# A transformer block with segmented attention: flips of the second layernorm by DMA for all of segment 0, a doubled tile written in one instruction, the gate inside the product, and a new timetable

## The chip, the cores and the metric

The kernel runs on one core of a Trainium2 chip. A core has TensorE (PE, matrix products into the eight PSUM banks), VectorE (DVE), ScalarE (ACT), GpSimd (POOL) and SyncE (SP, which issues DMAs), each with its own list of instructions that it works off in order; semaphores order them against each other. The metric is the time of one execution on the device in microseconds (us). The profile is one execution taken by the hardware profiler.

## The reference

One block on 2048 tokens of width 576, in bf16: attention, then an MLP of width 4608, both behind a layernorm and with a residual.

```python
q, k, v = x @ wq, x @ wk, x @ wv          # 32 heads of 18; 4 segments of 512 tokens
for s in range(4):                        # per segment, all heads
    p = softmax(qs @ ks.T * scale + causal_mask)
    a_dot = p @ vs
    a_mem = (phi(qs) @ M) / (phi(qs) @ z + 1e-6)
    o = g * a_mem + (1 - g) * a_dot       # g = sigmoid(beta), one number per head
    M, z = M + phi(ks).T @ vs, z + sum(phi(ks))
h  = x + concat(o) @ wo                   # x went through a layernorm before wq, wk, wv
h2 = h + gelu(layernorm(h) @ w1 + b1) @ w2 + b2
```

phi(t) is t + 1 for positive t and exp(t) otherwise. The memory M, z is empty in segment 0.

## The kernel before, in words

The 2048 tokens are four segments (s = 0 to 3) of four tiles of 128 tokens. The work of each segment goes through stages, and the letter and digits in front of a step's name give stage and segment (A1exp: an exp of stage A, segment 1). Where segment 0 is split, a third digit gives the tile (B01) or the pair of tiles (C00, C01).

- X (line 782): load of x, layernorm (line 733: stats, then rstd on GpSimd, then apply, which subtracts the mean and multiplies), and a transposed copy, by TensorE for the first pairs of tiles (line 771) and otherwise through DRAM and a transposing DMA ("flip", line 646).
- P (line 884): the products for q, k and v (line 865) and their eviction from PSUM (copy, line 652); for the memory phi(k) from ek (exp on ScalarE), rk (a clamp, line 932) and fk (line 934). q and k go to DRAM (qkst, line 918) and come back transposed (A1flip and so on). Within segment 0 the flips go from SBUF to SBUF.
- M (line 946): products and sums for the memory (macc, mblk).
- A (lines 1000 and 1130): scores (st, st0), exp on ScalarE, masks of the diagonal blocks (line 1196 on GpSimd, 1194 on VectorE; in segment 0 lines 1040 and 1037, with eight blocks in one instruction), the products with v (val), a transpose of the result on VectorE (valT), the reciprocal of the softmax sum and its multiplication by 1-g (rec2, lines 1218 to 1220), the product with the values (comb, line 1222) and the sum with the memory part (comb2). rg (line 1143) clamps q for phi(q); it stands on GpSimd.
- B (line 1244): the output projection (Po and Ro, line 826, in two halves that change banks between them, or "fused" into one where they follow each other), the residual (hadd), the second layernorm, and the transposed copy of its result. The tile xn2 has room for 2 x 576 columns: "tail" (line 1265) copies the 576 columns a second time behind the first, so that a flip gives nine blocks of 128 that hold each half of the rows twice. Tiles 2 and 3 of segment 0 and all tiles of segments 1 to 3 are flipped by DMA; tiles 0 and 1 of segment 0 are transposed on TensorE (line 777, steps B00T and B01T, 18 transposes in all, with four copies out of PSUM on VectorE), and there the tail copies 64 columns only.
- C (line 1286): the first MLP product (F1, lines 1312 and 1349; for segment 0 in two halves of 256 tokens, C00 and C01), eviction with the bias and gelu.
- D: the second MLP product (F2, line 1398), the residual with b2 (hc), the sum (oadd, line 1409) and the store.

The order is written out. TIMETABLE (line 22) gives each step, by name and number, its rank and its engine ("d 267": VectorE, rank 267; a row with one letter in front holds for all of its steps). The program builds all steps with their dependencies, sorts them by rank (schedule, line 402) and emits them in that order, so each engine's list is the ranks that carry its letter. The costs written beside each step (in us) and the tables OVER, PORT and SLIP only decide which buffer a step takes, by a model of the times. A DMA on SP waits in SP's list for what it reads, with all that stands behind it. The loads of x tiles 2 and 3 and of the q weights wait besides for a small copy, "gate" (line 724), that is made when the first half of x tile 0 has landed.

The functions that the change touches and those that call them:

## Time and profile before

| | |
|---|---|
| median of 3 runs | 449.36 us (448.22 to 450.42) |
| the profiled execution | 449.18 us, its span 447.5 us |
| HBM read and written | 37.36 MB and 10.29 MB |
| DMA issues of flips (transposing DMAs) | 54, all from SP |

In the rows of the profile a line begins with the line number of the kernel and the engine, then the operation, what it writes and what it reads ("bank<-xreg,w1g"), the shapes, and the count. Time behind a bar is busy time in all and the mean of one in ns; after a second bar stands how long the engine was idle just before and who ended that. PEld is the load of weights into TensorE, which overlaps the products.

### The profile page before, as it was taken

How to read it: one execution, taken by the hardware profiler on the slowest of the kernel's cores; microseconds unless marked ns; L12 is line 12 of the kernel's file. 1: busy time of each engine (PE TensorE's matmuls, PEld its weight loads, DVE VectorE, ACT ScalarE, POOL GpSimd, SP SyncE). 2: the span in 40 equal slices, each digit the busy share in tenths (PEclk: the TensorE clock that was granted, in tenths of full speed). 3: DMA queues.
4: the chain of work that ended last, by engine and by line, in shares of the span. 5: the costliest groups of instructions: out<-in, count | busy, mean ns of one | idle time of the engine just before them, and what ended most of it. 6: DMA issues, size and time to landing. Idle time of an engine off the chain costs nothing. (4 is left out here: it accounts for less than half of the span.)

```text
span 447.5 us, 12499 instructions
## 1 busy us (share of the span) xinstructions
PE 431.5 (96%) x5345; PEld 278.9 (62%) x5346; DVE 286.9 (64%) x623; ACT 301.2 (67%) x261; POOL 180.8 (40%) x319
## 2 busy tenths in 40 slices
PE   6987999899999999999999999999999999999997
PEld 4766677656776676664444766654447775445775
DVE  6899888999889877795678688773774322000012
ACT  6887999898978798775898977563787002566000
POOL 5683867668355833651235265520212111000001
PEclk9999999999999999999999999999999999999999
DMA  7669869999899944861657505404503281340001
GB/s 226 173 134 219 302 216 210 244 260 247 174 285 221 318 159 95 147 130 25 186 162 153 140 4 103 91 4 130 173 1 94 68 198 44 128 149 1 0 15 41
DMA packets 78344, 63.41 MB, mean 142 GB/s; under 512 B 62288, under 2 KB 70096, under 8 KB 78288
## 3 DMA queue, kind: packets, MB, share of 16 engines
q1 hardware_dynamic: 78144, 62.52, 54.9%
q8 instruction: 42, 0.69, 0.7%
q10 hardware_dynamic: 144, 0.09, 0.1%
q14 instruction: 14, 0.11, 0.1%
HBM read 37.36 MB, written 10.29 MB: 106 GB/s over the span
## 5 line engine op out<-in xcount | busy, mean ns | idle before, releaser
L1185 ACT ACTIVATE pt<-bank 128x2048 bf16<-128x2048 f32 x60 | 112.5, 1876 | 32.8 <-PE bank L1181 26.9
L1398 PEld LDWEIGHTS <-hT 128*128 128x128 bf16 x1152 | 110.5, 98 | 34.7 <-issue 6.6
L1312 PE MATMUL bank<-xreg,w1g 64*128 64x512 bf16 x972 | 107.2, 376 | 0.0
L1312 PEld LDWEIGHTS <-w1g 64*128 64x128 bf16 x972 | 46.3, 94 | 57.3 <-issue 2.8
L1398 PE MATMUL bank<-w_lo,hT 128*128 128x288 bf16 x576 | 77.8, 286 | 0.2 <-issue 0.2
L1398 PE MATMUL bank<-w,hT 128*128 128x288 bf16 x576 | 76.8, 286 | 0.6 <-DVE ot L1409 0.6
L1409 DVE TENSOR_TENSOR ot<-bank,hc 128x288 bf16<-128x288 f32 x32 | 14.3, 452 | 90.5 <-PE bank L1398 86.6
L873 PE MATMUL bank<-hT,xreg 64*128 64x288 bf16 x864 | 58.9, 283 | 4.8 <-DMA hT<-in_A_w_dram 2.1
L1196 POOL TENSOR_SCALAR_AFFINE_SELECT pt<-pt 128x512 bf16<-128x512 bf16 x67 | 45.1, 688 | 30.6 <-ACT pt L1185 30.3
L873 PEld LDWEIGHTS <-xreg 64*128 64x128 bf16 x864 | 42.8, 94 | 17.1 <-issue 8.5
L1317 ACT ACTIVATE hT<-bank,b_col 128x512 bf16<-128x512 f32 x36 | 22.6, 687 | 45.6 <-PE bank L1312 45.3
L1327 DVE TENSOR_SCALAR hT<-bank,b_col 128x512 bf16<-128x512 f32 x42 | 30.1, 742 | 21.4 <-PE bank L1312 20.2
L1384 POOL TENSOR_TENSOR hc<-h,b_bc 128x288 f32<-128x288 bf16 x16 | 12.4, 774 | 76.9 <-DVE ot L1409 76.9
L1027 ACT ACTIVATE pt<-bank 128x2048 bf16<-128x2048 f32 x20 | 37.5, 1877 | 6.2 <-PE bank L1024 5.5
L1349 PE MATMUL bank<-xreg,w1g 64*128 64x256 bf16 x648 | 38.6, 269 | 0.5 <-DVE qk_pad L662 0.3
L1349 PEld LDWEIGHTS <-w1g 64*128 64x128 bf16 x648 | 30.8, 94 | 7.0 <-issue 3.6
L1332 ACT ACTIVATE hT<-hT 128x8192 bf16<-128x8192 bf16 (+2 forms) x6 | 31.7, 5318 | 0.2 <-DVE hT L1327 0.2
L1325 ACT ACTIVATE hT<-bank,b_col 128x512 bf16<-128x512 f32 x30 | 19.5, 685 | 16.2 <-PE bank L1312 15.9
L1181 PE MATMUL bank<-qk 32*128 32x384 bf16 (+3 forms) x384 | 23.8, 300 | 1.6 <-DVE v_aug L662 0.9
L753 POOL TENSOR_SCALAR ln<-ln 128x1 f32<-128x1 f32 x32 | 8.8, 277 | 39.2 <-DVE ln L750 39.0
L1226 POOL TENSOR_TENSOR o_nat<-t,t 128x288 bf16<-128x288 f32 x13 | 10.6, 816 | 28.0 <-DVE t L1167 20.4
L1145 DVE SCALAR_TENSOR_TENSOR e<-e,r 128x512 bf16<-128x512 bf16 x24 | 18.9, 788 | 4.0 <-ACT e L1141 3.5
(119 smaller groups left out, 564.2 us busy)
## 6 DMA issues: line engine op xcount, KB each, us to landing
w1g<-in_B_w_dram SPq DMA_DIRECT2D x41, 576.0 KB, 4.4
qkd<-qk_pad SPq DMA_DIRECT2D x12, 512.0 KB, 4.8
w_lo<-in_B_w_dram SPq DMA_DIRECT2D x3, 864.0 KB, 6.6
w<-in_B_w_dram SPq DMA_DIRECT2D x3, 864.0 KB, 6.6
xb<-in_A_x_dram SPq DMA_DIRECT2D x16, 144.0 KB, 3.8
out_dram<-ot SPq DMA_DIRECT2D x15, 144.0 KB, 1.8
x<-in_A_x_dram SPq DMA_DIRECT2D x6, 320.0 KB, 4.5
xnd<-xn SPq DMA_DIRECT2D x10, 160.0 KB, 3.1
```

What stands on the lines that cost most here:

```text
L873: nc.tensor.matmul(out=c.t[:, w, 0:HALF], lhsT=xTb.t[r, k, ts], rhs=wt[r, k, :], start=(k == 0), stop=(k == ND - 1))
L1027: ex = add(ps, {"act": 1.88}, lambda e: nc.scalar.activation(out=pt.t[:], in_=st.t[:], func=ACT.Exp, scale=scale), [sc], pt, [st], table=" ...
L1181: nc.tensor.matmul(out=st.t[:, i, off:off + n_], lhsT=qk[rows, 1, kt * P:(kt + 1) * P], rhs=qk[rows, 0, kt * P:L], start=True, stop=True, ...
L1185: ex = add(ps, {"act": 1.88}, lambda e, st=st, pt=pt: nc.scalar.activation(out=pt.t[:], in_=st.t[:], func=ACT.Exp, scale=scale), [sc], pt, ...
L1196: nc.gpsimd.affine_select(out=blk, in_=blk, pattern=[[0, 4], [1, P]], compare_op=ALU.is_ge, fill=0.0, base=0, channel_multiplier=-1)
L1312: nc.tensor.matmul(out=cc[w].t[:], lhsT=w1.t[rows, k, q, :], rhs=x2T[s].t[rows, k, :], start=(k == 0), stop=(k == ND - 1))
L1317: ready_f[f + w] = [add(pf - 12, {"act": 0.68}, lambda e, f=f, w=w, cc=cc: nc.scalar.activation(out=hT[:, :, f + w, :], in_=cc[w].t[:].rea ...
L1325: nc.scalar.activation(out=dst, in_=src, func=ACT.Identity, bias=b)
L1327: nc.vector.tensor_scalar(out=dst, in0=src, scalar1=b, scalar2=None, op0=ALU.add)
L1332: ge = add(2.9, {"act": 0.42 * (f1 - f0) + 0.2}, lambda e, f0=f0, f1=f1: nc.scalar.activation(out=hT[:, :, f0:f1, :], in_=hT[:, :, f0:f1, ...
L1349: nc.tensor.matmul(out=cc[w].t[:, q * 2 * P:(q + 1) * 2 * P], lhsT=w1.t[rows, k, q, :], rhs=x2T[s].t[rows, k, ts], start=(k == 0), stop=(k ...
L1398: nc.tensor.matmul(out=c.t[:, 0:HALF], lhsT=hT[:, tl // 2, f, (tl % 2) * P:(tl % 2 + 1) * P], rhs=w2_c[ch][:, f - ch * WCH, hf * HALF:(hf ...
```

## The change

1. Tiles 0 and 1 of segment 0 are flipped by DMA as well: B00T, B01T and their copies go, B00flip and B01flip come.
2. The apply of the second layernorm writes both halves of the doubled tile in one instruction (twice=True: the input is read twice); all tail copies go. The apply may stand on GpSimd.
3. The multiplication by 1-g leaves rec2. On VectorE it is done within the product (scalar_tensor_tensor), on GpSimd it is an instruction of its own in front of the product.
4. rg and rk may stand on VectorE, the x applies on GpSimd; the masks of segment 0 are halved (four blocks in an instruction), and each half has its own engine.
5. A new timetable: nearly every rank is another, with new engines for small steps. The costs and the port model that choose the buffers are changed. By engine: 22 applies move to GpSimd (12 of x, 10 of h), 13 rg and 5 rk to VectorE, of the 32 half masks of segment 0 ten stand on VectorE.

The diff, cut to its core (of the timetable the rows that the text needs, of the numbers of the cost model nearly none):

```diff
-    "X00dma": "s 49 34 33",
-    "dma": "s 2 9 14 60 51 192 101 283",
-    "gate": "g 32",
-    "X1dma": "s 65 66 116 149",
+    "X00dma": "s 35 33 14",
+    "dma": "s 5 8 17 62 46 116 158 758",
+    "gate": "d 9",
+    "X1dma": "s 66 51 117 114",
...
-    "X01apply": "d 47 44",
-    "X1apply": "d 105 112 110 127",
+    "X01apply": "d52 g49",
+    "X1apply": "g 97 128 80 67",
...
-    "P1qkst": "s 263 209 313 314",
-    "A1flip": "s 341 426 349 410 501 502 529 632",
+    "P1qkst": "s 269 206 317 305",
+    "A1flip": "s 349 422 365 414 481 495 525 622",
...
-    "A00mask": "g 133 134 180 102",
-    "A02mask": "g 234 246 228 308",
+    "A00mask": "g113 d125 d111 g106 d120 d145 d156 g167",
+    "A02mask": "d252 g258 g259 g192 g225 d226 g298 d311",
...
-    "A1rg": "g 357 428 364 485 542 626 555 679",
+    "A1rg": "d375 g423 d366 g457 d592 g616 d623 d654",
...
-    "B00Po": "p 219",
-    "B00Ro": "p 223",
-    "B00T": "p 274 284",
-    "B00apply": "d 267",
-    "B00copy": "d 275 285",
-    "B00rstd": "g 266",
-    "B00tail": "g 273",
+    "B00Po": "p 222",
+    "B00Ro": "p 224",
+    "B00apply": "d 248",
+    "B00rstd": "g 238",
+    "B00flip": "s 249",
...
-    "B01Po": "p 225",
-    "B01Ro": "p 232",
-    "B01T": "p 276 286",
-    "B01apply": "d 256",
-    "B01copy": "d 277 287",
-    "B01rstd": "g 255",
-    "B01tail": "d 257",
+    "B01Po": "p 240",
+    "B01Ro": "p 245",
+    "B01apply": "g 273",
+    "B01rstd": "g 272",
+    "B01flip": "s 300",
...
-    "B1apply": "d 851 892 933 816",
-    "B2apply": "d 1213 1266 1292 1224",
+    "B1apply": "g 839 942 916 929",
+    "B2apply": "d1173 g1307 g1321 g1246",
...
-    "C00F1": "p 297 321 366 305 330 337 378 439 419",
-    "C00dma": "s 95 260 261 303 327 328 374 404 406",
+    "C00F1": "p 301 330 374 318 340 348 380 444 430",
+    "C00dma": "s 147 204 216 217 333 347 378 400 419",
...
-PARTS = dict(mask=1, apply=1, pq=1, fk=1, comb=1, comb2=1, memfin=1, hc=1, tail=1, swap=1)
-PORT = {"dve": PARTS, "pool": dict(PARTS, rg=1, rk=1, rstd=2, mblk=4, omg=4, gmz=1)}
+PORT = {"dve": dict(mask=(1, 0), pq=(1, 0), fk=(1, 0), comb=(1, 0), comb2=(1, 0), memfin=(1, 0), hc=(1, 0), rec0=(1, 0),
+                    apply=(1, 1), swap=(1, 1), rk=(1, 1), rg=(1, 1), mean=(1, 1), tail=(1, 1)),
+        "pool": dict(mask=(1, 0), pq=(1, 0), fk=(1, 0), apply=(1, 0), comb=(1, 0), comb2=(1, 0), memfin=(1, 0), hc=(1, 0), swap=(1, 0), rk=(1, 0), rg=(1, 0),
+                     rstd=(2, 0), mblk=(4, 0), omg=(4, 0), gmz=(1, 0), tail=(1, 0), memset=(1, 1), eps=(3, 1))}
...
-        def layernorm(prio, src, after, xsrc, dst_buf, dcost, extra=(), centred=None):
+        def layernorm(prio, src, after, xsrc, dst_buf, dcost, extra=(), centred=None, twice=False):
...
                 if centred is not None:
                     VEC[e].tensor_scalar(out=dst_buf.t[:, 0:w], in0=src(), scalar1=sm.t[:, mid:mid + 1], scalar2=None, op0=ALU.subtract)
                     return
-                VEC[e].tensor_scalar(out=dst_buf.t[:, 0:w], in0=src(), scalar1=sm.t[:, 12:13], scalar2=sm.t[:, 15:16], op0=ALU.subtract, op1=ALU.mult)
-            return add(prio, {"dve": dcost}, apply, (begun or [a, b]) + list(extra), dst_buf, [sm, xsrc], name="apply")
+                dst, frm = dst_buf.t[:, 0:w], src()
+                if twice:
+                    dst, frm = dst_buf.t[:].rearrange("p (n c) -> p n c", n=2), frm.unsqueeze(1).to_broadcast([P, 2, w])
+                VEC[e].tensor_scalar(out=dst, in0=frm, scalar1=sm.t[:, 12:13], scalar2=sm.t[:, 15:16], op0=ALU.subtract, op1=ALU.mult)
+            cost = {"dve": dcost} if centred is not None else {"dve": dcost, "pool": 1.28 if twice else 0.75}
+            return add(prio, cost, apply, (begun or [a, b]) + list(extra), dst_buf, [sm, xsrc], name="apply")
 
 
         xnT, xn_ok, applied = {}, {}, []
...
-                    b = add(p0 - 0.2, {"pool": 0.67}, lambda e, rk=rk, pad=pad: nc.gpsimd.tensor_scalar(
+                    b = add(p0 - 0.2, {"pool": 0.67, "dve": 0.36}, lambda e, rk=rk, pad=pad: VEC[e].tensor_scalar(
                         out=rk.t[:], in0=pad.t[:, :, 1, :, 0:Dh], scalar1=BIG, scalar2=0.0, op0=ALU.min, op1=ALU.max), ks, rk, [pad], name="rk")
-                    f = add(p0 - 0.2, {"dve": 0.78}, lambda e, ek=ek, rk=rk, fk=fk: nc.vector.scalar_tensor_tensor(
+                    f = add(p0 - 0.2, {"dve": 0.76}, lambda e, ek=ek, rk=rk, fk=fk: nc.vector.scalar_tensor_tensor(
...
                 for u in range(0, len(diag), 2):
-                    o0, w = diag[u][4], diag[u][3]
-
-                    def mask(e, o0=o0, w=w):
-                        blk = pt.t[:, :, o0:o0 + 2 * w].rearrange("p i (b q) -> p i b q", q=w)[:, :, :, 0:P]
-                        if e == "dve":
-                            nc.vector.tensor_tensor(out=blk, in0=blk, in1=tri[:].unsqueeze(1).unsqueeze(1).to_broadcast([P, 4, 2, P]),
-                                                    op=ALU.mult)
-                        else:
-                            nc.gpsimd.affine_select(out=blk, in_=blk, pattern=[[0, 4], [0, 2], [1, P]], compare_op=ALU.is_ge, fill=0.0,
-                                                    base=0, channel_multiplier=-1)
-                    masks[u] = add(ps, {"dve": 0.87, "pool": 1.17}, mask, [ex, tri_ok], None, [pt], name="mask")
-                    masks[u].bias = {"dve": MASK_BIAS}
+                    for i0 in (0, 2):
+                        o0, w = diag[u][4], diag[u][3]
+
+                        def mask(e, o0=o0, w=w, i0=i0):
+                            blk = pt.t[:, i0:i0 + 2, o0:o0 + 2 * w].rearrange("p i (b q) -> p i b q", q=w)[:, :, :, 0:P]
+                            if e == "dve":
+                                nc.vector.tensor_tensor(out=blk, in0=blk, in1=tri[:].unsqueeze(1).unsqueeze(1).to_broadcast([P, 2, 2, P]),
+                                                        op=ALU.mult)
+                            else:
+                                nc.gpsimd.affine_select(out=blk, in_=blk, pattern=[[0, 2], [0, 2], [1, P]], compare_op=ALU.is_ge, fill=0.0,
+                                                        base=0, channel_multiplier=-1)
+                        masks[u, i0] = add(ps, {"dve": 0.43, "pool": 0.64}, mask, [ex, tri_ok], None, [pt], name="mask")
+                        masks[u, i0].bias = {"dve": MASK_BIAS}
                 return [(4 * Q + b, kt, q0, n_, off, pt) for (b, kt, q0, n_, off) in units], [ex] + list(masks.values())
 
             def values(tag, t0, parts, banks, acq, cost):
...
-                a = add(prio - 0.2, {"dve": 0.48}, c0, [a] + later, r1, [t1], name="rec")
...
-                b = add(pg, {"pool": 0.64}, lambda e, g=g, rb=rb: nc.gpsimd.tensor_scalar(
+                b = add(pg, {"pool": 0.62, "dve": 0.30}, lambda e, g=g, rb=rb: VEC[e].tensor_scalar(
...
 
                 def c0(e, g=g, r1=r1, t1=t1):
                     nc.vector.reciprocal(out=r1.t[:], in_=t1.t[:, :, Dh])
-                    nc.vector.tensor_scalar(out=r1.t[:], in0=r1.t[:], scalar1=omg_q[:, g:g + 1], scalar2=None, op0=ALU.mult)
-
-                def c1(e, r1=r1, t1=t1):
-                    VEC[e].tensor_tensor(out=t1.t[:, :, 0:Dh], in0=t1.t[:, :, 0:Dh], in1=r1.t[:].unsqueeze(2).to_broadcast([P, 16, Dh]), op=ALU.mult)
-                a = add(pc, {"dve": 0.53}, c0, [a] + later, r1, [t1], name="rec2")
-                a = add(pc, {"dve": 0.48, "pool": 0.70}, c1, [a], None, [r1, t1], name="comb")
-                a = add(pc, {"dve": 0.52, "pool": 0.87}, lambda e, g=g, t1=t1: VEC[e].tensor_tensor(
+
+                def c1(e, g=g, r1=r1, t1=t1):
+                    rb = r1.t[:].unsqueeze(2).to_broadcast([P, 16, Dh])
+                    if e == "dve":
+                        nc.vector.scalar_tensor_tensor(out=t1.t[:, :, 0:Dh], in0=t1.t[:, :, 0:Dh], scalar=omg_q[:, g:g + 1], in1=rb, op0=ALU.mult, op1=ALU.mult)
+                        return
+                    nc.gpsimd.tensor_scalar(out=r1.t[:], in0=r1.t[:], scalar1=omg_q[:, g:g + 1], scalar2=None, op0=ALU.mult)
+                    nc.gpsimd.tensor_tensor(out=t1.t[:, :, 0:Dh], in0=t1.t[:, :, 0:Dh], in1=rb, op=ALU.mult)
+                a = add(pc, {"dve": 0.26}, c0, [a], r1, [t1], name="rec2")
+                a = add(pc, {"dve": 0.46, "pool": 0.90}, c1, [a] + later, None, [r1, t1], name="comb")
+                a = add(pc, {"dve": 0.46, "pool": 0.82}, lambda e, g=g, t1=t1: VEC[e].tensor_tensor(
                     out=o_q(on)[:, :, Dh * g:Dh * g + Dh], in0=t1.t[:, :, 0:Dh], in1=t2s[g].t[:, :, 0:Dh], op=ALU.add),
                     [a, t2_ok[g]] + done[:1], on if g == 0 else None, [t1, t2s[g]] + ([on] if g else []), name="comb2")
                 done.append(a)
...
                         out=h.t[:, cs], in0=c.t[:, 0:HALF], in1=xb.t[:, cs], op=ALU.add), [a, ld, prev], h if hf == 0 else None,
                         [c, xb] + ([] if hf == 0 else [h]), name="hadd")
                 xn2 = Buf(xn2_s)
-                ap = layernorm(p0, lambda h=h: h.t[:], [prev], h, xn2, 0.48, later)
-                by_dma = s > 0 or tl in DMA_FLIP_0
-                w = D if by_dma else 64
-                ap = add(p0, {"pool": 0.72, "dve": 0.38} if by_dma else {"pool": 0.29, "dve": 0.22},
-                         lambda e, xn2=xn2, w=w: VEC[e].tensor_copy(out=xn2.t[:, D:D + w], in_=xn2.t[:, 0:w]), [ap], None, [xn2], name="tail")
+                ap = layernorm(p0, lambda h=h: h.t[:], [prev], h, xn2, 0.60, later, twice=True)
                 h_ok[t] = h, prev
-                if by_dma:
-                    x2_ok[s].append(flip(p0, lambda tl=tl: x2T[s].t[:, :, tl * P:(tl + 1) * P], lambda xn2=xn2: xn2.t[:], ND,
-                                         [ap] + (x2_ok[s][:1] if tl else p3_done), None if tl else x2T[s], [xn2] + ([x2T[s]] if tl else [])))
-                else:
-                    even = transposes(p0, xn2, [ap], lambda tl=tl: x2T[s].t[:, 0:KT, tl * P:(tl + 1) * P],
-                                      x2T[s] if tl == 0 else None, [] if tl == 0 else [x2T[s]])
-                    if tl:
-                        even.after.append(x2_ok[s][0][0])
-                    odd = transposes(p0, xn2, [ap], lambda tl=tl: x2T[s].t[:, KT:ND, tl * P:(tl + 1) * P], None, [x2T[s]], ND - KT, c0=64)
-                    odd.after.append(even)
-                    x2_ok[s].append([even, odd])
+                x2_ok[s].append(flip(p0, lambda tl=tl: x2T[s].t[:, :, tl * P:(tl + 1) * P], lambda xn2=xn2: xn2.t[:], ND,
+                                     [ap] + (x2_ok[s][:1] if tl else p3_done if s else []), None if tl else x2T[s], [xn2] + ([x2T[s]] if tl else [])))
 
         f2_chunks = {}
         last_w1 = [None]
...
-        DMA_FLIP_0 = (2, 3)
...
```

More of the change, by code (lines that the diff above doesn't have):

```diff
@@ L477, in schedule, with meet @@
         return order
+    @staticmethod
+    def meet(e, kind, other):
+        dve, pool = (kind, other) if e == "dve" else (other, kind)
+        return bool(dve) or not pool
     @staticmethod
```

43 lines of the change are left out of this document (22 added, 21 removed), and 527 rows, old and new, of the table TIMETABLE.

## The prediction

> **What bounds the kernel now.** I read the page's head and then the table of busy time by stretches (columns: stretch, its length, then busy us and instructions of PE, PEld, DVE, ACT and POOL, the granted clock, the DMA share and GB/s).
>
> ```profile
> span 447.5 us, 12499 instructions
> PE 431.5 (96%) x5345; PEld 278.9 (62%) x5346; DVE 286.9 (64%) x623; ACT 301.2 (67%) x261; POOL 180.8 (40%) x319
> ...
> 0.00:120.00 120.00, 108.14 (x1913) 77.47 (x1913) 106.61 (x235) 103.84 (x97) 79.97 (x157) 1.00 0.88 221
> 120.00:440.00 320.00, 318.99 (x3402) 198.16 (x3400) 178.99 (x385) 197.34 (x165) 100.06 (x161) 1.00 0.45 115
> 440.00:447.50 7.50, 4.38 (x36) 3.26 (x34) 1.28 (x3) 0.00 (x0) 0.73 (x1) 1.00 0.10 32
> ```
>
> TensorE is the bound: of 16.0 us in which it has nothing, 11.9 lie in the first 120 us (120.00 - 108.14), 1.0 in the next 320 and 3.1 at the end (the last addition and the store). The clock is 1.00 throughout. VectorE and ScalarE are nearly full in that first stretch (106.6 and 103.8 of 120) and have room later. The chain of waits, in order of time, says the same of the last part:
>
> ```profile
> 373.92 35.07 PE bank L1312 x324
> 408.99 35.40 PE bank L1398 x288
> ```
>
> Product follows product with nothing between. So an edit late in the kernel gains only where it takes instructions off TensorE, and an edit early gains what it takes out of the waits before 120 us. Those are in the waits of TensorE (total, times, longest):
>
> ```profile
> PE bank L873 <- DMA hT<-in_A_w_dram: 2.1, 1, 2.1
> PE bank L873 <- DVE qk_pad L662: 1.8, 3, 1.0
> PE bank L1024 <- DVE MZacc L968: 1.7, 1, 1.7
> ...
> PE bank L1024 <- ACT pt L1027: 1.3, 4, 0.4
> PE bank L1181 <- DVE v_aug L662: 0.9, 1, 0.9
> ...
> PE bank L873 <- DVE v_aug L662: 0.5, 1, 0.5
> ...
> PE bank L1349 <- DVE qk_pad L662: 0.3, 1, 0.3
> ```
>
> One wait is for weights at the start. Five rows are waits for VectorE to empty a bank: 1.8 + 1.7 + 0.9 + 0.5 + 0.3 = 5.2 us.
>
> **The transposes of tiles 0 and 1.** They go from TensorE to DMA flips.
>
> ```profile
> 55.56 1.27 PE L777 MATMUL bank<-ident,xn 128*128 128x128 bf16 x18
> 56.76 0.61 PE L1056 MATMUL bank<-pt,v_aug 128*19 128x256 bf16 x16
> 57.67 0.40 PE L1024 MATMUL bank<-w_lo 32*128 32x256 bf16 x8 [0.30 <-ACT pt L1027]
> ```
>
> The 18 transposes hold the engine from 55.56 to 56.76: 1.20 us, and the value step after them does not depend on them. Lower bound 0.9: the step at 57.67 already waits 0.30 for an exp, and would meet it earlier. Since TensorE is full afterwards, the gain is kept. I take **-1.2**. Changes between the ways of cutting the array (64 rows, 32 rows, 32 columns, whole) cost TensorE nothing net: counting them in both lists gives 215 before and 215 after, with four fused output projections in both.
>
> **VectorE before 120 us.** The rows are groups by form (busy us, mean ns) and, for the x apply, minimum, median and maximum of one:
>
> ```profile
> L765 DVE TENSOR_SCALAR xn<-x,ln 128x640 bf16<-128x640 bf16 x14 | 9.3, 670 | 0.6 <-POOL ln L754 0.5
> L765 DVE TENSOR_SCALAR xn<-h,ln x16: 348/428/837, 52.6 to 365.4; 128x576 bf16<-128x576 bf16 x16
> L765 DVE TENSOR_SCALAR xn<-x,ln x14: 392/442/1231, 9.4 to 99.6; 128x640 bf16<-128x640 bf16 x14
> L1220 DVE TENSOR_SCALAR r<-r,omg_q 128x16 f32<-128x16 f32 x24 | 7.0, 290 | 0.9
> L662 DVE COPY xreg<-bank 128x640 bf16<-128x640 bf16 x5 | 2.3, 483 | 0.8 <-PE bank L777 0.8
> L1194 DVE TENSOR_TENSOR pt<-pt,tri 128x512 bf16<-128x512 bf16 x29 | 14.9, 527 | 1.1 <-ACT pt L1185 1.1
> L1037 DVE TENSOR_TENSOR pt<-pt,tri 128x1024 bf16<-128x1024 bf16 x2 | 1.4, 678 | 0.0
> L1266 POOL COPY xn<-xn 128x576 bf16<-128x576 bf16 x7 | 4.8, 689 | 5.4 <-DVE xn L765 5.4
> ```
>
> I counted both lists up to the first product of C01. Off VectorE: 12 of the 14 x applies (12 x 0.67 = 8.0), two h applies (2 x 0.43 = 0.9), four copies after the transposes (4 x 0.45 = 1.8), three masks of A1 (3 x 0.53 = 1.6), four multiplications by 1-g (4 x 0.29 = 1.2): 13.5. Onto it: ten half masks of segment 0, priced as the A1 mask, which is as large, for two whole ones (10 x 0.53 - 2 x 0.68 = 3.9), and seven of the small clamps rg and rk, priced as the nearest row, the h apply (7 x 0.43 = 3.0): 6.9. Net about -6.6 of 106.6, so its idle time in the stretch grows from 13.4 to about 20 us. The gate multiplied within the product costs VectorE at least nothing more (the same 128 x 288 elements) and at most the 0.29 that it saves; from GpSimd's side it is one more 128 x 16 instruction where the product stands there.
>
> GpSimd takes the 12 x applies at about 0.77 each (the 0.689 of its 576-wide copy, times 640/576): an estimate. It is busy for 80 of the 120 us, so it has the room. A doubled apply lies between one and two of the plain ones: 0.43 to 0.86 on VectorE, 0.7 to 1.4 on GpSimd, where it replaces apply and tail together; I take 0.6 and 1.3. Late, in segments 1 to 3, both engines have idle time and TensorE does not wait for them, so I put all that at nothing; its cover is the 320 us stretch with 1.0 us of TensorE idle, and without that cover each doubled apply on GpSimd would cost its flip 0.9.
>
> What this buys is read at two waits, in the order of time of VectorE and of TensorE:
>
> ```profile
> 22.72 2.28 DVE L765 TENSOR_SCALAR xn<-x,ln 128x640 bf16<-128x640 bf16 x2
> 24.92 0.74 DVE L662 CAST qk_pad<-bank 128x576 bf16<-128x576 f32 x1
> ...
> 25.72 2.38 PE L873 MATMUL bank<-hT,xreg 64*128 64x288 bf16 x36 [1.00 <-DVE qk_pad L662]
> ...
> 28.92 1.28 PE L873 MATMUL bank<-hT,xreg 64*128 64x288 bf16 x18 [0.48 <-DVE v_aug L662]
> ```
>
> Two x applies, stretched to 1.14 us each, stand in front of the eviction that TensorE waits for. They leave the engine, so I count these waits as gone: 1.48. Of the other 3.7 I take a quarter, 0.9, between nothing and the half by which the idle time grows. Sum **-2.4**, bounds 0 and -5.2. What is late next is ScalarE: it keeps its work (and gets two swaps more) and its 1.3 us row of waits stays.
>
> The clamp A1rg on VectorE waits for the flips of A1; behind it in VectorE's list stand the eviction P1copy.8, a reciprocal and the evictions of C00, for whose banks TensorE waits. The flips are issued well ahead, so I put this at nothing; its bound is in the range.
>
> **The order of the first loads.** The second part of the k weights (the third load of the list "dma") is put behind the x tile 3, and that one waits for the gate.
>
> ```profile
> 1.73 0.90 SPq L640 DMA_DIRECT2D hT<-in_A_w_dram  x2
> 3.62 0.80 SPq L640 DMA_DIRECT2D x<-in_A_x_dram  x2
> 4.46 0.43 SPq L640 DMA_DIRECT2D hT<-in_A_w_dram  x1
> ...
> hT<-in_A_w_dram SPq DMA_DIRECT2D x1, 288.0 KB, 4.4
> ...
> 11.01 2.38 PE L873 MATMUL bank<-hT,xreg 64*128 64x288 bf16 x36 [2.06 <-DMA hT<-in_A_w_dram]
> ```
>
> Today it leaves at about 2.2. Behind the gate it leaves at about 4.0 and lands at 8.4, so the second half of the first k projection waits for some 1.2 us. That fits into the 2.06 us wait for the q weights. But these leave one issue (0.43) later. I take **+0.3**, bounds 0 and +0.9: the v weights are behind an x load of segment 1 too.
>
> **The flips of tiles 0 and 1 on the path to the first product of C00.**
>
> ```profile
> 47.91 0.66 PE L832 MATMUL bank<-wt_o,oT 64*128 64x288 bf16 x8
> 52.62 0.38 DVE L765 TENSOR_SCALAR xn<-h,ln 128x576 bf16<-128x576 bf16 x1
> 54.34 0.43 DVE L765 TENSOR_SCALAR xn<-h,ln 128x576 bf16<-128x576 bf16 x1 [0.37 <-POOL ln L754]
> 58.00 2.14 PE L1349 MATMUL bank<-xreg,w1g 64*128 64x256 bf16 x36
> ...
> xreg<-xn SPq DMA_TRANSPOSE x14, 3.6
> ```
>
> From the start of the last output projection of tile 1 to the first product of C00 pass 10.1 us today. The new list has a projection more in between and no transposes, about the same. The new chain is 5.1 us to the end of the earlier apply, or 6.9 to the end of the later one, then 3.6 for the flip, and up to 0.9 for the longer apply on GpSimd: 8.7 to 11.4. So the product waits between nothing and 1.3 us: I take **+0.3**.
>
> **Sum.** 449.18 us is the profiled execution's own time (span 447.5): 449.18 - 1.2 - 2.4 + 0.3 + 0.3 = 446.2. The median of the three runs, 449.36, is 0.18 above the profiled one, so the forecast is **446.4 us**.
>
> **Rivals.** *The larger gain*: all of the 5.2 us goes and neither new wait shows: 449.36 - 1.2 - 5.2 = 443.0. For it: four of the five rows are single waits, which a new order can remove whole. Against: ScalarE, at 103.8 of 120, keeps its pace.
>
> *The relief is eaten*: the x apply has a median of 442 ns and a maximum of 1231, and the two at 22.72 ran beside GpSimd. If the applies on GpSimd hold VectorE up in their turn, each meeting costs 1.23 - 0.44 = 0.79; from eight meetings on, among the 14 applies that go there early, the 6.6 us are used up. Then 449.36 - 1.2 + 0.6 = 448.8. The Trainium skill (SBUF — State Buffer, section SBUF: two separate sides) says that VectorE in its two-port forms and GpSimd take a shared port pair as an exclusive lock for a whole instruction; by that rule this rival would hold, and the 1231 ns agree with it. Against the rival: the applies that ran into this on VectorE are the ones that leave it.
>
> *Slower*: the flip of tile 1 becomes the wait. Its apply stands on GpSimd behind two masks of A02, and an rstd and an apply of X2, then its own rstd. A GpSimd instruction beside VectorE is stretched too:
>
> ```profile
> L1040 POOL TENSOR_SCALAR_AFFINE_SELECT pt<-pt x14: 1101/1112/1617, 18.7 to 75.6; 128x1024 bf16<-128x1024 bf16 x14
> ```
>
> With 0.5 us more (1.617 - 1.112) for each of six instructions, the wait in front of C00's first product becomes 1.3 + 3.0 = 4.3. On SP the two stores of P1, a load of X3, two of w1 and the first flip of A1 stand behind that flip, so the scores of segment 1 are late as well and the relief is not collected: 449.36 - 1.2 + 0.3 + 4.3 = 452.8. It decides from a wait of 3.1 us on.
>
> **How the numbers follow.** About 0.5% (2.25 us) is what a measurement of this kernel can tell from no change: below 447.1 is faster, above 451.6 slower. Forecast 0.52, larger gain 0.10, relief eaten 0.25, slower 0.13. Of the forecast's 0.52 I put 0.42 below 447.1 and 0.10 above. Faster 0.42 + 0.10 = 0.52; same 0.10 + 0.25 = 0.35; slower 0.13. The range leaves out the slower rival and half of the larger gain: 443.0 to 450.2.
>
> **What would show it.** In the changed profile: no transposes between the scores of A02 and the first product of C00; PE busy about 430.3; VectorE in the first 120 us near 100; the rows L662 of TensorE's waits at about half; the x applies on GpSimd at 0.75 to 0.8, or at 1.2 and more if the relief is eaten; the first product of C00 preceded by a wait below 1.3 for a DMA into xreg. I am wrong if TensorE's idle time before 120 us is still 11 us or more, or if new waits appear after 120 us.

## The result and the profile after

The changed kernel takes 479.44 us (median of 4 runs, 477.80 to 482.65) against 449.75 for the kernel before on the same chips: a ratio of 1.067, with an interval from 1.061 to 1.074. The forecast was 446.4 with a range up to 450.2, so it missed by 33 us and in sign. The profiled execution took 477.8 us, its span 476.1.

The head of the page:

```profile
span 476.1 us, 12461 instructions
PE 439.2 (92%) x5328; PEld 283.2 (59%) x5328; DVE 295.2 (62%) x583; ACT 303.2 (64%) x267; POOL 245.5 (52%) x338
```

The table of busy time by stretches (its columns as in the prediction):

```profile
0.00:120.00 120.00, 99.47 (x1681) 69.90 (x1682) 91.06 (x204) 92.40 (x92) 96.44 (x155) 0.94 0.80 198
120.00:440.00 320.00, 306.75 (x3384) 187.14 (x3383) 198.44 (x366) 209.54 (x174) 147.62 (x182) 0.99 0.44 124
```

GpSimd went from 180.8 to 245.5 us. VectorE's busy time rises too, from 286.9 to 295.2, though it has 40 instructions fewer; a row below shows why. TensorE idles for 20.5 us of the first 120 (11.9 before) and for 13.3 of the next 320 (1.0 before). VectorE and ScalarE do less before 120 us, not more (91.1 and 92.4, from 106.6 and 103.8): they wait, like TensorE. The granted clock is below 1 in both stretches. GpSimd's own groups by form say where its 65 us come from:

```profile
L766 POOL TENSOR_SCALAR xn<-h,ln 128x1152 bf16<-128x1152 bf16 x10 | 43.4, 4336 | 0.7
L766 POOL TENSOR_SCALAR xn<-x,ln 128x640 bf16<-128x640 bf16 x12 | 30.3, 2525 | 1.1
```

An x apply takes 2.53 us there and a doubled one 4.34. The prediction had 0.77 and 1.3. The 22 applies sum to 73.7 us instead of 22. In the waits of TensorE (total, times, longest) two kinds are new, waits for GpSimd and waits for a VectorE that is itself late because of GpSimd:

```profile
PE bank L1210 <- POOL pt L1199: 4.6, 5, 1.3
PE bank L1059 <- DVE qk_pad L660: 4.4, 1, 4.4
PE bank L779 <- POOL xn L766: 3.6, 1, 3.6
...
PE bank L1306 <- DMA xreg<-xn: 0.9, 1, 0.9
```

The last row is a flip of a later segment, at 324 us. The first product of C00 (L1343, at 65.87) did not wait for its flips here: it comes right behind the gap of 4.4 us, so this trace does not test the 0 to 1.3 of the prediction. The order of time shows both new kinds:

```profile
30.25 2.52 POOL L766 TENSOR_SCALAR xn<-x,ln 128x640 bf16<-128x640 bf16 x1
...
32.83 0.37 PE L779 MATMUL bank<-ident,xn 128*128 128x128 bf16 x3 [3.60 <-POOL xn L766]
...
57.43 4.29 POOL L766 TENSOR_SCALAR xn<-h,ln 128x1152 bf16<-128x1152 bf16 x1
58.05 4.73 DVE L935 TENSOR_SCALAR rk<-qk_pad 128x576 bf16<-128x576 bf16 x1
...
61.66 0.95 POOL L634 MEMSET MZ_blk<- 128x1024 bf16 x1
...
64.36 1.03 PE L1059 MATMUL bank<-pt,v_aug 128*19 128x256 bf16 x16 [4.39 <-DVE qk_pad L660]
```

At 30.25 TensorE's transposes wait directly for an x apply. At 57.43 a doubled apply starts; a clamp that VectorE otherwise does in some 0.3 us starts 0.6 later and ends at 62.78, when the apply (to 61.72) and the memset behind it (to 62.61) are over. I call this a hold. The eviction behind the clamp is late, and TensorE with it. After both gaps the granted clock falls. In short stretches (the clock is the third number from the end) it is 1.00 while TensorE has little or nothing to do, and 0.50 as soon as it works again:

```profile
28.00:32.00 4.00, 1.11 (x27) 0.82 (x25) 1.86 (x4) 3.78 (x4) 3.81 (x5) 1.00 1.27 138
34.00:36.00 2.00, 2.00 (x18) 1.03 (x14) 1.78 (x5) 0.00 (x0) 2.00 (x4) 0.50 1.22 268
60.00:62.00 2.00, 0.00 (x0) 0.00 (x0) 2.00 (x1) 0.75 (x1) 2.00 (x2) 1.00 0.00 0
66.00:68.00 2.00, 2.00 (x22) 1.36 (x20) 1.22 (x6) 2.00 (x2) 2.00 (x3) 0.50 0.59 229
```

My first theory after this was: the applies on GpSimd are too dear, and they cost time by holding VectorE up. The rival: they cost time because GpSimd itself gets late with all that stands behind them. A second rival: not the applies, but the new order.

### The profile page after: what moved, and what is told of

It reads as the page before. It is cut to its first block, busy times and chain, and to the rows that moved or that the text cites. A ratio compares the mean times of both kernels' runs of the same rounds, so it can differ in the third digit from the quotient of the medians.

```text
span 476.1 us, 12461 instructions
## 1 busy us (share of the span) xinstructions
PE 439.2 (92%) x5328; PEld 283.2 (59%) x5328; DVE 295.2 (62%) x583; ACT 303.2 (64%) x267; POOL 245.5 (52%) x338
## 5 line engine op out<-in xcount | busy, mean ns | idle before, releaser
L1306 PEld LDWEIGHTS <-w1g 64*128 64x128 bf16 x972 | 47.6, 94 | 58.8 <-issue 5.1
L1392 PE MATMUL bank<-w,hT 128*128 128x288 bf16 x576 | 78.3, 288 | 1.1 <-DVE t L1164 0.8
L1199 POOL TENSOR_SCALAR_AFFINE_SELECT pt<-pt 128x512 bf16<-128x512 bf16 x74 | 51.8, 714 | 41.6 <-ACT pt L1188 41.4
L1311 ACT ACTIVATE hT<-bank,b_col 128x512 bf16<-128x512 f32 x36 | 22.4, 688 | 47.9 <-PE bank L1306 47.8
L1378 POOL TENSOR_TENSOR hc<-h,b_bc 128x288 f32<-128x288 bf16 x11 | 8.3, 756 | 82.0 <-DVE ot L1403 82.0
L766 POOL TENSOR_SCALAR xn<-h,ln 128x1152 bf16<-128x1152 bf16 x10 | 43.4, 4336 | 0.7
L1321 DVE TENSOR_SCALAR hT<-bank,b_col 128x512 bf16<-128x512 f32 x39 | 27.6, 739 | 23.5 <-PE bank L1306 18.6
L1343 PE MATMUL bank<-xreg,w1g 64*128 64x256 bf16 x648 | 40.4, 278 | 0.1
L1343 PEld LDWEIGHTS <-w1g 64*128 64x128 bf16 x648 | 31.6, 97 | 7.6 <-issue 3.0
L1319 ACT ACTIVATE hT<-bank,b_col 128x512 bf16<-128x512 f32 x33 | 20.8, 685 | 19.7 <-PE bank L1306 19.6
L766 POOL TENSOR_SCALAR xn<-x,ln 128x640 bf16<-128x640 bf16 x12 | 30.3, 2525 | 1.1
```

The source lines that it names most:

```text
L766: VEC[e].tensor_scalar(out=dst, in0=frm, scalar1=sm.t[:, 12:13], scalar2=sm.t[:, 15:16], op0=ALU.subtract, op1=ALU.mult)
L1199: nc.gpsimd.affine_select(out=blk, in_=blk, pattern=[[0, 4], [1, P]], compare_op=ALU.is_ge, fill=0.0, base=0, channel_multiplier=-1)
L1306: nc.tensor.matmul(out=cc[w].t[:], lhsT=w1.t[rows, k, q, :], rhs=x2T[s].t[rows, k, :], start=(k == 0), stop=(k == ND - 1))
L1311: ready_f[f + w] = [add(pf - 12, {"act": 0.68}, lambda e, f=f, w=w, cc=cc: nc.scalar.activation(out=hT[:, :, f + w, :], in_=cc[w].t[:].rea ...
L1321: nc.vector.tensor_scalar(out=dst, in0=src, scalar1=b, scalar2=None, op0=ALU.add)
L1343: nc.tensor.matmul(out=cc[w].t[:, q * 2 * P:(q + 1) * 2 * P], lhsT=w1.t[rows, k, q, :], rhs=x2T[s].t[rows, k, ts], start=(k == 0), stop=(k ...
```

## The experiments

**All applies back on VectorE**, and then only the x or only the h applies, at the same ranks (the program picks the buffers anew from its cost model, so a few of these may differ as well):

```
-    "X1apply": "g 97 128 80 67",
+    "X1apply": "d 97 128 80 67",
...
-    "B1apply": "g 839 942 916 929",
+    "B1apply": "d 839 942 916 929",
```

> All 22 applies that the change put on GpSimd stand on VectorE again, at the same ranks; everything else is the changed kernel. Theory (price of the apply): on GpSimd it takes 2.52 us (x) and 4.34 us (doubled h) instead of my 0.77 and 1.3, and holds VectorE meanwhile; without that the time falls from 479 to 446-450, and TensorE's idle time to about 16 us. Rival (order): the new order itself is worse and the long applies only show up in it; then 465 or more.

Measured 449.14 us, 1.0007 times the kernel before (0.9987 to 1.0028): the loss is gone, and so the order by itself is not the cause. TensorE idles for 15.4 us (447.0 - 431.6), as expected. But nothing is left of the gain either.

> Only the 12 x applies go back to VectorE; the 10 doubled h applies stay on GpSimd. TensorE's time beyond its products and changes of mode is 28.4 us before 125 us in the changed kernel against 15.1 in the one before, and 17.8 against 1.0 after that. Theory: the x applies are 10 of the 12 us early, so 467-470; the late waits stay. Rival (order): less than 5 us off. Rival (h alone matters): no change within 2 us.

Measured 471.12 (1.045 to 1.053): 8.3 us come back with 12 x applies, 1.1 short of the range expected.

> Only the 10 doubled h applies go back to VectorE; the 12 x applies stay on GpSimd. Theory: the waits after 125 us go, 17 us, and those behind tile 1 of segment 0 too, so 457-462. If the two groups cost independently of each other, the gains of this kernel and of the one with the x applies alone add up to that of both.

Measured 461.48 (1.025 to 1.030): 18.0 us come back with 10 doubled h applies, as expected. The two sum to 26.3 of 30.3, so they are nearly, not quite, independent. TensorE's idle time says where each group costs: with the h applies back it is 20.5 us before 120 and 0.8 from 120 to 440, with the x applies back 14.8 and 12.4. Most of the loss is in the doubled applies, of which eight stand in segments 1 to 3, where the prediction had put everything at nothing.

**Why an apply is slow on GpSimd.** Twelve of the 22 places got another form of instruction:

```
+                if form == "ii":    # two constants, subtract and multiply
+                    VEC[e].tensor_scalar(out=dst, in0=frm, scalar1=0.0, scalar2=1.0, op0=ALU.subtract, op1=ALU.mult)
...
+                elif form == "mm":  # two constants, minimum and maximum
+                    VEC[e].tensor_scalar(out=dst, in0=frm, scalar1=3.0, scalar2=-3.0, op0=ALU.min, op1=ALU.max)
```

> The changed kernel with other forms of the apply at 12 of the 22 places on GpSimd (the normalization is left out or only half done there), to read the duration of each form: two immediates, a pointer and an immediate, one pointer, one immediate, min and max with immediates, max and min with pointers, two tensor_tensor with the scalar broadcast. Theory (pointer): a scalar from SBUF per partition is what is slow; immediates take about 0.77 us for 640 and 1.3 for 1152, one pointer is slow as two or half as slow. Rival (operation): subtract and mult are slow in any form and min/max is fast in any form. Rival (lock): all forms at one place take the same, because the instruction waits for VectorE.

The groups by form, for 640 columns: L787 is the kernel's own form (mean and root by pointer, subtract and multiply), L772 two constants with subtract and multiply, L782 maximum and minimum with both by pointer, L776 a subtract by pointer alone, L778 a multiply by a constant alone, L784 one tensor_tensor with a broadcast operand, L780 minimum and maximum with constants.

```profile
L787 POOL TENSOR_SCALAR xn<-x,ln 128x640 bf16<-128x640 bf16 x4 | 10.1, 2536 | 0.3
L772 POOL TENSOR_SCALAR xn<-x 128x640 bf16<-128x640 bf16 x2 | 4.7, 2372 | 0.2
...
L782 POOL TENSOR_SCALAR xn<-x,ln 128x640 bf16<-128x640 bf16 x1 | 2.5, 2507 | 0.1
...
L776 POOL TENSOR_SCALAR xn<-x,ln 128x640 bf16<-128x640 bf16 x1 | 1.9, 1901 | 0.0
L778 POOL TENSOR_SCALAR xn<-x 128x640 bf16<-128x640 bf16 x1 | 1.8, 1841 | 0.1
L784 POOL TENSOR_TENSOR xn<-x,ln 128x640 bf16<-128x640 bf16 x1 | 1.3, 1256 | 0.0
...
L780 POOL TENSOR_SCALAR xn<-x 128x640 bf16<-128x640 bf16 x1 | 0.7, 716 | 0.0
```

Each of these is one instruction over the same 640 columns, and the tensor_scalar alone takes between 0.72 and 2.54 us. Neither the pointer nor the operation explains it alone: constants with subtract and multiply are slow (2.37), and so are pointers with maximum and minimum (2.51). Only minimum and maximum with constants come near the price of the prediction, at 1.1 ns a column against 4.0. None of the three expectations holds as it stands. The forms stood at different places, most of them once; but in the changed kernel the own form takes 2.51 to 2.58 us at all twelve x places, and in the next experiment the fast form takes 0.71 to 0.98 at the same twelve, so neither the place nor waiting for VectorE explains the difference. What GpSimd does longer in the slow forms stays open. The clamps (rk, 0.67 us for 576 columns) and the copies (0.69) are of the fast kind, and it was from a copy that the prediction took its price.

**The forecast with the price that it assumed.** All 22 applies on GpSimd in the fast form, which leaves the normalization out, so that this is a measurement and no usable kernel:

```
-                VEC[e].tensor_scalar(out=dst, in0=frm, scalar1=sm.t[:, 12:13], scalar2=sm.t[:, 15:16], op0=ALU.subtract, op1=ALU.mult)
+                if e == "pool":
+                    VEC[e].tensor_scalar(out=dst, in0=frm, scalar1=3.0, scalar2=-3.0, op0=ALU.min, op1=ALU.max)
...
```

> The changed kernel with the 22 applies left on GpSimd in their places, but as a minimum and a maximum with constants instead of subtract and multiply (the normalization is left out there): 0.72 us for 640 columns and 1.14 us for the doubled 1152, where the changed kernel's own take 2.5 and 4.3. These are close to the prices of the prediction (0.77 and 1.3). Theory (the price of the apply on GpSimd is the whole miss, and all else was read rightly): 446 to 450 us. If the relief of VectorE before 120 us is real, 446 to 447; if it isn't, as the kernel with all applies on VectorE suggests, 448 to 450. Rival (the order of the new timetable is itself too tight once GpSimd has this work, whatever the price): 455 us or more.

Measured 443.56 us, a ratio of 0.9865 (0.9844 to 0.9886), 2.4 below the range expected. The head of its page:

```profile
PE 430.6 (97%) x5328; PEld 277.1 (63%) x5328; DVE 270.3 (61%) x583; ACT 302.4 (68%) x267; POOL 192.1 (43%) x338
```

GpSimd's groups by form:

```profile
L767 POOL TENSOR_SCALAR xn<-h 128x1152 bf16<-128x1152 bf16 x10 | 11.8, 1184 | 0.0
L767 POOL TENSOR_SCALAR xn<-x 128x640 bf16<-128x640 bf16 x12 | 9.0, 748 | 0.1
```

And the first 120 us of the table by stretches:

```profile
0.00:120.00 120.00, 112.05 (x1972) 78.88 (x1974) 101.50 (x231) 108.25 (x104) 83.32 (x172) 1.00 0.98 226
```

With 20.8 us of applies on GpSimd instead of 73.7, TensorE idles for 8.0 us before 120 (11.9 before the change), it is busy for 430.6 in all (the prediction said 430.3), and VectorE does 101.5 there (near 100). The rows of waits for VectorE's evictions are down to 0.3 and 0.2 us. The time is near that of the larger gain, 443.0. So the other steps of the prediction hold taken together, and the difference to the changed kernel, 35.9 us, is the price of 53 us of GpSimd: 0.68 us for each, on average.

**Held or late?** First the applies in pieces:

```
+                step = w if e == "dve" else 144 if twice else 128
+                for c in range(0, w, step):
...
```

> The changed kernel with each apply on GpSimd cut into pieces of 128 columns (640 columns in 5 pieces) or 2 x 144 columns (the doubled tile in 4 pieces): the same arithmetic on the same engine, in pieces of some 0.5 and 1.1 us. Theory (VectorE's instructions that meet a running apply are held until it ends, by up to 4.4 us, and that is most of the 30 us): between two pieces VectorE gets its turn, so no VectorE instruction is stretched by more than about 1.2 us, and the time falls to 455 to 465 us. Rival (GpSimd's own work is late: its sums of 73.7 us push the masks and gates that TensorE waits for): the time stays at 476 to 486 us, since the pieces sum to as much or more.

Measured 507.96 us (1.128 to 1.132): worse by 28.5, where my theory said better and the rival much the same. The pieces do not scale down:

```profile
L769 POOL TENSOR_SCALAR xn<-h,ln 128x288 bf16<-128x288 bf16 x40 | 54.7, 1377 | 0.6
L769 POOL TENSOR_SCALAR xn<-x,ln 128x128 bf16<-128x128 bf16 x60 | 49.2, 832 | 1.1
```

A quarter of a doubled apply takes 1.38 us (a quarter of 4.34 is 1.08), a fifth of an x apply 0.83 (instead of 0.51), so each further instruction costs some 0.4 us ((5 x 0.83 - 2.53) / 4 and (4 x 1.38 - 4.34) / 3), and the applies now sum to 103.9 us. The holds beside the applies are gone: the masks of segments 1 to 3, which VectorE does in 0.42 us, took at most 0.87, and 3.55 in the changed kernel. VectorE is busy for 269.5 us, against 295.2 in the changed kernel with as many instructions. One long hold is left, and it stands beside a row of GpSimd's masks, none longer than 0.7 us:

```profile
41.07 4.18 POOL L1046 TENSOR_SCALAR_AFFINE_SELECT pt<-pt 128x512 bf16<-128x512 bf16 x7
...
42.27 4.51 DVE L1043 TENSOR_TENSOR pt<-pt,tri 128x512 bf16<-128x512 bf16 x1
```

Less time held and more time in all: that speaks for the rival. In the chain of work that ended last GpSimd has 27% here, and 2% with all applies on VectorE. But two things had changed at once. So the next run kept GpSimd's total and took only the long instructions away: the fast form, three or four times over (here too the normalization is left out). The sentence in its expectation that the pieces held VectorE nowhere for over 1 us overlooks the row above.

```
+                    for _ in range(4 if twice else 3):
+                        VEC[e].tensor_scalar(out=dst, in0=frm, scalar1=3.0, scalar2=-3.0, op0=ALU.min, op1=ALU.max)
```

> The changed kernel with its 22 applies on GpSimd as a minimum and a maximum with constants (normalization left out there), each of them issued several times over: 4 times for the doubled tile (4 x 1.14 = 4.6 us, where the changed kernel's one takes 4.3), 3 times for 640 columns (3 x 0.72 = 2.2 us, instead of 2.5). GpSimd is thus as late as in the changed kernel (71 us of applies instead of 74), but no single instruction of it runs longer than some 1.2 us, so VectorE cannot be held longer than that. Theory now (GpSimd's own lateness is the price; the instructions in pieces held VectorE nowhere for over 1 us and still took 508 us): 474 to 480 us. Rival (the holds of up to 4.7 us on VectorE are most of it): 450 to 460 us.

Measured 481.54 us (1.069 to 1.075), 1.5 above the range that the theory gave and far from the rival's. GpSimd's groups by form:

```profile
L768 POOL TENSOR_SCALAR xn<-h 128x1152 bf16<-128x1152 bf16 x40 | 48.7, 1216 | 2.5
L768 POOL TENSOR_SCALAR xn<-x 128x640 bf16<-128x640 bf16 x36 | 27.2, 756 | 2.1
```

The waits of TensorE:

```profile
PE bank L1214 <- POOL pt L1203: 9.6, 5, 4.3
PE bank L783 <- POOL xn L768: 4.3, 1, 4.3
```

And the clamp rk on VectorE, which took 4.73 us above (minimum, median and maximum of one, in ns):

```profile
L939 DVE TENSOR_SCALAR rk<-qk_pad x4: 281/521/824, 9.9 to 100.8; 128x576 bf16<-128x576 bf16 x4
```

75.9 us of applies instead of 73.7, and 481.5 us instead of 479.4, a difference within the scatter of the runs. The long holds are gone (this clamp takes 0.82 at most, those masks 1.39, and VectorE is busy for 279.0 us instead of 295.2; with the fast form once it was 270.3) and the time is the same. What TensorE waited for through VectorE, it now waits for directly: the masks' row has gone from 4.6 to 9.6, and two waits for flips behind late applies are 2.7 and 2.2. My theory of the hold falls as the main price; a few microseconds of it could hide in the difference of the two runs. What costs is that GpSimd's list is in order, and the masks and the roots of variance that the next products need stand behind the applies.

**The parts of the forecast by themselves.** The flips of tiles 0 and 1 in the kernel before, put into SP's list at ranks 276.5 and 277.5 (I tried no other place):

```
-        DMA_FLIP_0 = (2, 3)
+        DMA_FLIP_0 = (0, 1, 2, 3)
...
```

> The kernel before with one part of the change alone: the second flips of tiles 0 and 1 of segment 0 by DMA, their 18 transposes on TensorE and 4 evictions on VectorE left out; bank numbers of the matmuls pinned to those of before. Prediction's terms: 1.2 us less of TensorE (bounds 0.9 to 1.2), 0.3 us more of waiting in front of the first C00 product (0 to 1.3): 448.5 us, between 448.2 and 449.5. Rival (the flip of tile 1 is late and the products wait): 450 us or more.

Measured 457.28 us (1.015 to 1.019), the rival. In its order of time:

```profile
56.59 3.70 SPq L649 DMA_TRANSPOSE xreg<-xn  x2
...
61.51 0.43 SPq L642 DMA_DIRECT2D x<-in_A_x_dram  x1
...
62.35 3.64 PE L1347 MATMUL bank<-xreg,w1g 64*128 64x256 bf16 x36 [2.88 <-DMA xreg<-xn]
...
66.56 0.82 DVE L751 BATCH_NORM_STATS2 ln<-x 128x6 f32<-128x288 bf16 x2 [8.02 <-DMA x<-in_A_x_dram]
```

In the old order the flips leave SP at 56.6, the first product waits for them, and the load of x behind them on SP comes so late that VectorE waits 8 us for it. That is the slower rival of the prediction in its outline, a late flip with other loads behind it on SP, though here the applies stand on VectorE and it is two flips that fill SP. Of the 8.7 us between the spans (456.2 and 447.5), 3.3 are TensorE's own busy time (434.8 against 431.5), as the granted clock fell to 0.50 three times, twice of them from the gap at 62 us on. In the new order the wait in front of this product is 0.6 us with all applies on VectorE, inside the 0 to 1.3 of the prediction, and none with the fast form. A part that loses 8 us by itself can be harmless within its timetable.

**The warm-up tile's memset first again**, on top of all applies on VectorE:

```
-    "memset": "d1 d23 g40 g22 d0 a91 a41 a43 a162 g407 g201 g276",
+    "memset": "d0 d23 g40 g22 d1 a91 a41 a43 a162 g407 g201 g276",
```

> The kernel with all applies on VectorE, with one more thing put back: VectorE's memset of the warm-up tile again stands before the memset of the column of ones in the values. Theory (the swap delays the warm-up matmuls by 0.5 us, and these stand in front of the second tile's transposes, so that tile 0's projections begin at 7.42 instead of 6.57 us): 448.3 to 448.9 us against 449.1, with the first matmul at 1.28 us again. Rival (the loads of the weights set the pace of the head anyway): 449.1, nothing gained.

Measured 449.05 us (0.998 to 1.001): no difference. The first matmul starts 0.5 us earlier, and then TensorE waits 1.5 us for the weights into hT, which it did not wait for noticeably in the kernel that this edits. The rival is right in the time: what the head gained, the wait for the loads took.

**Is there a version that beats both?** GpSimd got VectorE's clamps (13 rg and four rk; it is four that the change moves, not five), a fast form, and five masks instead of the applies:

```
-    "P2rk": "d427 g513 g549 g564",
+    "P2rk": "g 427 513 549 564",
...
-    "A3rg": "g1038 g1042 g1201 g1100 g1110 d1260 d1361 d1344",
+    "A3rg": "g 1038 1042 1201 1100 1110 1260 1361 1344",
```

> The kernel with all applies on VectorE (449.1 us), and the small work that the new timetable gave to VectorE put on GpSimd in its stead: all 17 clamps rk and rg (0.26 to 0.3 us each on VectorE, 0.6 to 0.7 on GpSimd) and the 5 masks of the first attention step; bank numbers pinned. Theory (what the cheap applies gained beyond 449.1 is VectorE's time before 125 us, 3 us of it between 12 and 23 us, and clamps are a form that GpSimd does fast): 445 to 448 us, a version faster than both kernels. Rival (the clamp is on the path there, and its 0.35 us more on GpSimd lengthen it as much as VectorE gains): 449 to 451 us.

Measured 452.83 us (1.007 to 1.012), beyond the rival. No wait for GpSimd stands at the top of TensorE's list; new near it are one for VectorE's e (1.3) and one for the weights (1.4). The order of time shows what the first of them is:

```profile
148.01 1.19 POOL L1146 TENSOR_SCALAR r<-qk 128x512 bf16<-128x512 bf16 x2
148.66 1.09 DVE L1148 SCALAR_TENSOR_TENSOR e<-e,r 128x512 bf16<-128x512 bf16 x1 [2.52 <-POOL r L1146]
149.80 0.38 PE L1155 MATMUL bank<-e,MZ_blk 128*128 128x512 bf16 x1 [1.34 <-DVE e L1148]
```

VectorE waits 2.5 us for a clamp that GpSimd now does, and TensorE for VectorE: the rival's mechanism, in one place. It is 1.3 of the 4 us; I did not trace the rest.

Then two of the x applies, and in a second run four, against all on VectorE:

```
-    "X1apply": "d 97 128 80 67",
-    "X2apply": "d 227 270 280 292",
+    "X1apply": "d97 d128 g80 g67",
+    "X2apply": "g227 g270 d280 d292",    (the second run only)
```

> The kernel with all applies on VectorE, except that two keep the changed kernel's place on GpSimd, at 2.5 us each: those of the x tiles 2 and 3 of segment 1, which are flipped by DMA and are waited for some 20 us later; the arithmetic is the reference's. Theory (TensorE's idle 3.0 us between 12 and 23 us with all on VectorE come from VectorE's queue, and GpSimd is idle for 7 of these 11 us, so that a slow apply is free there where nothing near waits for it or for what stands behind it): 446.5 to 448.5 us, faster than both kernels. Rival (the masks, clamps and roots of variance behind the two applies on GpSimd are late by as much): 449 to 452 us.

Measured 450.90 us (1.002 to 1.006), the rival.

> As the one before, and the applies of x tiles 0 and 1 of segment 2 stay on GpSimd too, at 2.5 us each. Theory (VectorE is busy for 34 of the 37 us from 23 to 60, GpSimd for 23, and these tiles too are flipped by DMA and read much later): another 0 to 1 us less, 446 to 448 us. Rival (between 23 and 60 us GpSimd's masks are on the path, and each apply in front of one delays it by up to 2.5 us): 451 to 455 us.

Measured 453.40 us (1.008 to 1.012). The rival again. In both, one wait of TensorE for the eviction of v on VectorE (3.6 and 4.0 us) is new, and with four applies one of 2.7 for another eviction. With two applies the order of time shows how the first comes about:

```profile
19.33 2.52 POOL L757 TENSOR_SCALAR xn<-x,ln 128x640 bf16<-128x640 bf16 x1
...
22.12 0.57 POOL L743 TENSOR_TENSOR ln<-ln,mhalf 128x1 f32<-128x1 f32 x1
...
22.72 0.45 DVE L757 TENSOR_SCALAR xn<-x,ln 128x640 bf16<-128x640 bf16 x1 [3.95 <-POOL ln L743]
...
24.68 0.75 DVE L651 CAST v_aug<-bank 128x576 bf16<-128x576 f32 x1
...
25.48 1.77 PE L866 MATMUL bank<-hT,xreg 64*128 64x288 bf16 x26 [3.59 <-DVE v_aug L651]
```

The root of variance of the next tile stands behind the slow apply on GpSimd. VectorE's own apply waits for that root for 3.95 us, with nothing held, and the eviction of v stands behind it in VectorE's list. This is lateness without a hold, handed from list to list. Even two slow applies in an idle stretch of GpSimd cost more than they free. I found no version with the reference's arithmetic that beats the kernel before.

## Why the prediction was wrong

- **The step that failed: the price of the apply on GpSimd.** "GpSimd takes the 12 x applies at about 0.77 each (the 0.689 of its 576-wide copy, times 640/576): an estimate", and for the doubled one "0.7 to 1.4". It measured 2.53 and 4.34. A copy has no arithmetic and no operand by pointer; the price of an instruction was scaled from one of another kind, and the bounds were made from the same row, so they could not contain the error. Even a row of the same opcode would have confirmed the wrong price: the clamp rk, a tensor_scalar on 128 x 576, took 0.67 us on GpSimd. The profile before had rows of arithmetic on GpSimd, such as the product with the values, tensor_tensor on 128 x 288 in 0.709 us. At that rate 640 columns take 1.6 us and 1152 take 2.8: still too little, but with it the upper bound of the applies would have been 47 us of GpSimd (12 x 1.6 + 10 x 2.8) instead of 23 (12 x 0.77 + 10 x 1.4), and at the 0.68 us for each that the runs gave, the range would have reached beyond 460.
- **"It is busy for 80 of the 120 us, so it has the room."** Busy for 96 of 120 us, GpSimd still idles for 24, and what it does late delays the others all the same. Room in the sum is not room in front of the next mask.
- **"Late, in segments 1 to 3 ... I put all that at nothing."** TensorE's idle time from 120 to 440 us went from 1.0 to 13.3. The cover was named, but its breadth was taken from TensorE's idle time, which tells nothing of how late GpSimd may be. The doubled applies, eight of ten of them there, are the larger part of the loss.
- **The relief of VectorE, -2.4 (0 to -5.2), and the flips, -1.2 and +0.3.** With the assumed price the kernel takes 443.56 us: 5.9 less than before. The sum of the prediction's terms was -3.0. The same timetable with all applies on VectorE, 449.14, is no faster than the kernel before, so the quick applies on GpSimd alone bring 5.6 and the other terms together about nothing, where the prediction had -0.6. The relief was thus taken too small, -2.4 where the runs give about its bound of -5.2, and it was there only as long as GpSimd was quick.
- **The rival of the hold.** The Trainium skill (SBUF — State Buffer, section SBUF: two separate sides) states that the loser of the shared port pair waits for the whole instruction of the other. The trace agrees: 4.73 us for a clamp beside an apply of 4.29. It also shows holds beyond one instruction: this one lasts to the end of the memset behind the apply, and the 4.51 us in the run of the pieces stand beside instructions of 0.7 us at most. The prediction priced a meeting at 0.79 because the instruction that holds was taken to be as short as before. And yet the runs without long instructions show that these holds are not where most of the time went.
- **The slower rival** was one mechanism, a late flip. The flips alone, put into the old order, show it; in the new order the wait is 0.6 us or none, unless the doubled apply in front of the flip takes four instructions (2.7).
- The sentence "I am wrong if TensorE's idle time before 120 us is still 11 us or more, or if new waits appear after 120 us" was met on both counts: 20.5 us, and 13.3.

## What to carry to other kernels

Price an instruction that changes its engine by a row of that engine with the same operation and the same kind of operands; where the trace has none, let the bound be several times the nearest row, and ask what the sum would be at that end. Idle time of an engine whose list is in order is no room: ask which instruction stands behind the new one, and who waits for it. When a hold and a delay both appear in a trace, keep the engine's total and cut its instructions short: if the time stays, the hold was mostly where the delay became visible.

## What the runs showed of the hardware

- GpSimd's tensor_scalar on bf16 has a fast form, minimum and maximum with constants (0.72 us for 640 columns, 1.14 for 1152), and slow ones: 1.84 to 1.90 us with one operation, 2.37 to 2.54 with two, whether arithmetic with constants or minimum and maximum with pointers. The Trainium skill (GPSIMD Engine Reference, section 4.1 Engine selection) calls instructions with one input roughly line-rate there; the fast form, at 1.1 ns a column, is nearest to that, the others are up to 3.5 times slower than it, and the measurement decides.
- Each further piece of a cut apply on GpSimd cost 0.4 us.
- Of the 34.2 us between the spans of the changed kernel and of the one with the fast form, 8.7 are TensorE's own busy time (439.24 against 430.57), with as many instructions: the granted clock fell to 0.50 four times. Counted in stretches of 1 us, each with what its clock lacks to 1, the falls after the gaps of 3.6 and 4.4 us cost 1.7 and 3.4 us (an estimate), so these stalls are paid for twice. The Trainium skill (TensorE: Matmul & The Clock Gate, section Part 1: The HAM clock gate) puts the fall to half at an idle window of some 3.4 us, and both gaps are longer than that. The other two falls, of 1.7 us each by the same count, are not explained by that: from 12 to 16 us, with no wait of TensorE before it longer than 1.65 us, and from 217 to 221 us, after waits of 2.9 and 0.8 us.
